# Linear attention with a GELU MLP behind it: the second group's output in seven products, and the last group's stores cut in halves

## The chip, the cores and the metric

The kernel runs on one core of a Trainium2 chip. The metric is the device time of one execution in microseconds. The five engines of the core run side by side: TensorE (PE in the profile) multiplies matrices into PSUM, VectorE (DVE) and ScalarE (ACT) work elementwise, GpSimd (POOL) does a few casts here, and SyncE (SP) issues most DMAs. Each works through its own queue of instructions in order and waits on semaphores for the others.

## What is computed

```python
# q, k, v: 8 batches, 8 heads, 576 rows, 64 wide
phi = lambda x: where(x > 0, x, exp(x) - 1) + 1
q_p, k_p = phi(q), phi(k)
kv  = einsum('bhsd,bhse->bhde', k_p, v)
z   = sum(k_p, axis=2)
x   = einsum('bhsd,bhde->bhse', q_p, kv) / (einsum('bhsd,bhd->bhs', q_p, z)[..., None] + 1e-06)
x   = x.transpose(0, 2, 1, 3).reshape(4608, 512)
h   = x @ w_in                      # 512 -> 2048
g   = gelu_tanh(h)
out = g @ w_out                     # 2048 -> 512
```

## The kernel before

**Tiling.** The 4608 rows are taken in nine groups. Groups 0 to 7 are the first 512 rows of batches 0 to 7; group 8 is made of the last 64 rows of all eight batches. `iteration(j)` does group j: `h` in 16 blocks of 128 features by 512 rows (four matmuls each, into one PSUM bank), a gelu per block on ScalarE into `g`, and then `o`, the product of `g` with `w_out`. The attention of a group that comes later (its exps, its kv, its division and its transposes) is done in between, so that TensorE is never without work.

**Two forms of o.** Groups 0 and 1 multiply plainly: per quarter of 128 rows, 16 matmuls with 512 columns (`o_mm`, line 723), and a copy to `o_sb` by ScalarE or VectorE (`finish`). In group 1 half of them stand after the first eight h, the other half after the last eight. Groups 2 to 8 cut `g` and `w_out` into two by two blocks and form `o` from seven products and not eight (`class Products`): each has 16 matmuls with 256 columns (`product`, line 770), some on sums of blocks of `g` (`s[0]`, `s[1]` and two blocks of `g` overwritten in place, line 752) and on differences of blocks of `w_out` (`w_sum` and one block of `w_out_sb` overwritten, `sum_w_out`, line 741). The results are put together by VectorE additions from PSUM (`plus`, line 830) and two ScalarE copies. Three of the products, 2, 4 and 3, are added by TensorE to a bank that already holds another one (`p`, `w`, `z`), so these banks stay taken for some time, and an addition that reads such a bank has to be done before TensorE adds to it again.

**PSUM.** There are six single banks (`ps_b`) for h, o, transposes and some of the attention, and one pair of banks (`ps_a`) for kv and for `n` of the attention, the numerator and denominator of one quarter of the rows (`nab`; `nab_in_banks` takes two single banks instead).

**The order.** Nothing is scheduled by the compiler: each engine executes in the order in which the program writes its instructions. `steps` in `iteration` lists the h blocks and products of a group, and after step number `slot` the function `run(j, slot)` calls what `at(j, slot, ...)` has put there. `plan_third` and `plan_fourth` put the attention of batches 2 and 3 into group 1 and the start of group 2:

- `linear_of` (VectorE, line 228) and `exp_of` (ScalarE, line 220) are the two branches of phi, `least_of` (VectorE, line 234) their minimum. The exp tiles `q_e` and `k_e` exist once each. `gelu_table` (line 418) brings ScalarE's gelu table back after exps.
- `least_q` takes the minimum for q and then issues four DMA transposes `qt<-q_p` on SP's queue (line 660); `transposed_x` issues one `xt<-xs` per quarter (line 683).
- `load_all_pairs` and `load_q` issue loads on SP's queue.
- `cast_v`, `kv_in_pair` and the `n` steps follow.
- `attention` of batch 3 stands in group 2 after slot 12 (line 328) and uses four single banks and the pair.

**Stores.** In groups 0 to 7 ScalarE's queue issues the stores of `o`. Group 8 stores through `store_rest` (line 834), alternately from ScalarE's queue and SP's: the left half of `o1`, all of `o2` (both column halves at once, after product 4), and the right half of `o1` in two pieces at the very end.

Of the kernel before, what the change touches and what calls it, by code (L numbers as in the profile page):

```python
# [16 lines left out]
def kernel(  # L17
# [28 lines left out]
    MM = d_ff // P  # L46
    E = D + 1
    N2 = d_model // 2
# [337 lines left out]
    xts, qts = {}, {}  # L386
# [126 lines left out]
    def at(j, slot, fn, *args):  # L513


        fill.setdefault((j, slot), []).append((fn, args))
# [73 lines left out]

    def plan_third():
        def n(c):
            transposed_x(2, c, nab(qts[2], 2, c))

        for i, name in enumerate("qk"):
            at(1, 2 + i, linear_of, name, 2)
            at(1, 7, exp_of, name, 2)
        at(1, 4, cast_v, 2)
        at(1, 7, gelu_table)
        at(1, 9, least_q, 2)  # L600
        at(1, 10, load_all_pairs, "k", k, 4)
        at(1, 11, least_of, "k", 2)
        at(1, 16, kv_in_pair, 2)
        for c in range(C):
            at(1, 18 + 2 * c, n, c)

    def plan_fourth():

        for name, b in (("k", 3), ("q", 3), ("k", 4)):
            at(1, 23, exp_of, name, b)  # L610
        at(1, 23, gelu_table)
        at(1, 24, linear_of, "k", 3)
        at(1, 25, linear_of, "q", 3)
        at(1, 26, least_of, "k", 3)
        at(1, 31, least_q, 3)
        at(2, 0, cast_v, 3)
        at(2, 4, kv_in_pair, 3)
        at(2, 5, linear_of, "k", 4)
        at(2, 5, least_of, "k", 4)
        at(2, 5, cast_v, 4)  # L620
        at(2, 8, linear_of, "q", 4)
        at(2, 15, exp_of, "q", 4)
        at(2, 16, exp_of, "k", 5)
        at(2, 19, least_q, 4)
        at(2, 22, linear_of, "k", 5)
        at(3, 0, least_of, "k", 5)
# [53 lines left out]
    def transposed_x(b, c, x):  # L680
        if b not in xts:
            xts[b] = pt.tile([P, NP, MAIN], BF16, name="xt")
        nc.sync.dma_start_transpose(out=xt_chunk(b, c), in_=x)
# [50 lines left out]
    def sum_w_out(ns):  # L734

        b11, b21 = (w_out_sb[:, 0, h] for h in ff)
        b12, b22 = (w_out_sb[:, 1, h] for h in ff)
        t1, t2, t4 = (w_sum[:, n] for n in range(3))
        sums = ((t1, b12, b11), (t2, b22, t1), (t4, b21, t2), (b12, b22, b12))
        for out, i0, i1 in sums[ns]:  # L740
            nc.vector.tensor_tensor(out, i0, i1, op=ALU.subtract)

# [2 lines left out]
    class Products:  # L745
# [5 lines left out]
        def subtract(self, out, i0, i1, op=ALU.subtract):  # L751
            nc.vector.tensor_tensor(out, i0, i1, op=op)  # L752

        def sums(self, ms):

            (a11, a12), (a21, a22) = [[h[:, ms] for h in t] for t in self.a]
            s1, s2 = (s[:, ms] for s in self.s)
            self.subtract(s1, a21, a22, ALU.add)
            self.subtract(s2, s1, a11)
            self.subtract(a21, a11, a21)  # L760

        def last_sum(self):

            self.subtract(self.a[0][0], self.a[0][1], self.s[1])

        def product(self, ps, lhs, rhs, first, ts=range(2)):

# [8 lines left out]
                        skip_group_check=True,  # L776
                    )

        def step(self, n):
            j = self.j  # L780
            (a11, a12), (a21, a22) = self.a
            (b11, b21), (t3, b22) = [[w_out_sb[:, d, h] for h in ff] for d in range(2)]
            t1, t2, t4 = (w_sum[:, i] for i in range(3))
            lo, hi = slice(0, N2), slice(N2, d_model)
            if n == 1 and j == B:
                ps = [bank("o_ps", [P, N2]) for _ in range(2)]
            elif n < 4:
                ps = bank("o_ps", [P, 2, N2])
            if n == 0:
                self.p = ps  # L790
                self.product(ps, a11, b11, True)
                self.o1 = pout.tile([P, 2, d_model], FP32, name="o_sb")
                self.o2 = pout.tile([P, 2, d_model], FP32, name="o_sb")
                nc.scalar.copy(self.o1[:, :, hi], ps)
            elif n == 1:
                self.z = ps
                self.product(ps, self.s[0], t1, True)
            elif n == 2:
                self.product(ps, self.s[1], t2, True)
                self.plus(self.o1[:, :, hi], ps, self.o1[:, :, hi])  # L800
            elif n == 3:
                self.w = ps
                self.product(ps, a21, t3, True)
                self.plus(self.o2[:, :, hi], ps, self.o1[:, :, hi])
                if j < B:
                    self.plus(self.o2[:, :, hi], self.z, self.o2[:, :, hi])
                else:
                    for t in range(2):
                        self.plus(self.o2[:, t, hi], self.z[t], self.o2[:, t, hi])
            elif n == 4:  # L810
                self.product(self.p, a12, b21, False)
                nc.scalar.copy(self.o1[:, :, lo], self.p)  # L812
                if j == B:
                    self.store(0, self.o1, lo)
            elif n == 5:
                self.product(self.w, a22, t4, False)
                self.plus(self.o2[:, :, lo], self.w, self.o1[:, :, hi])
                self.store(1, self.o2)
            elif j < B:
                self.product(self.z, a11, b22, False)  # L820
                self.plus(self.o1[:, :, hi], self.z, self.o1[:, :, hi])
                at(j + 1, 0, self.store, 0, self.o1)
            else:
                for t in range(2):
                    self.product(self.z, a11, b22, False, (t,))
                    self.plus(self.o1[:, t, hi], self.z[t], self.o1[:, t, hi])
                    self.store_rest(t, self.o1[:, t], hi)

        def plus(self, out, i0, i1):
            nc.vector.tensor_tensor(out, i0, i1, op=ALU.add)  # L830
# [17 lines left out]
    def iteration(j):  # L848
        xt = xts[j]
        if j < B:  # L850
            g = pg.tile([P, 2, MM, MAIN // 2], FP16, name="g")
        else:
            g = pg.tile([P, MM, 2, MAIN // 2], FP16, name="g").rearrange("p m a n -> p a m n")
        hs = [("h", m) for m in range(MM)]
        us = [range(m, m + 4) for m in range(0, MM, 4)]
        if j == 0:
            us[2:3] = range(8, 10), range(10, 12)
            steps = hs + [("o", t, u) for u in us for t in range(C)]
        elif j == 1:
            os = [[("o", t, u) for u in us[i : i + 2] for t in range(C)] for i in (0, 2)]  # L860
            steps = hs[:8] + os[0] + hs[8:] + os[1]
        else:
            products = Products(j, g)
            steps = [hs[i + n] for i in range(MM // 2) for n in (0, MM // 2)]
            steps += [("product", n) for n in range(7)]
            at(j, 7, products.sums, slice(0, 4))
            at(j, 15, products.sums, slice(4, 8))
            at(j, 16, products.last_sum)
        o_pss = {}
        for slot, step in enumerate(steps):  # L870
            if step[0] == "h":
                m = step[1]
                h_ps = h_begun.get(j, {}).get(m)
                if h_ps is None:
                    h_ps = bank("h_ps", [P, MAIN])
                    h_mm(h_ps, xt, m)
                gelu(j, g, m, h_ps)
            elif step[0] == "product":
                products.step(step[1])
            else:  # L880
                t, u = step[1:]
                if u.start == 0:
                    o_pss[t] = bank("o_ps", [P, d_model])
                o_mm(o_pss[t], g, t, u, half=(j, slot - 0.5))
                if u.stop == MM:
                    finish(j, t, o_pss[t])
            run(j, slot)
# [7 lines left out]
        plan_rest(m)  # L895
    for b in range(3, B + 1):
        plan_attention(b)
    at(1, 26, load_all_pairs, "v", v, 4)
    at(1, 26, load_q, 4)
    for b in range(5, B):  # L900
        at(b - 3, 1, load_all_pairs, "k", k, b)
        at(b - 3, 1, load_q, b)
# [3 lines left out]
        at(5, 1, load_rest, m + 2)  # L906
    for j in range(2, 7):
        at(j, 16, gelu_table)
    at(1, 4, sum_w_out, slice(0, 3))
    at(2, 0, sum_w_out, slice(3, 4))  # L910

    for j in range(B + 1):
        iteration(j)
# [30 lines left out]
```

## Time and profile before

| what | value |
|---|---|
| median of 8 runs | 273.5 us (273.27 to 273.77) |
| the profiled execution's own time | 273.47 us |
| its span, first to last instruction | 271.7 us |
| granted TensorE clock, mean | 0.997 |
| end of the last TensorE work in the chain of waits | 267.2 us |
| start of group 1's h in the chain / of group 2's | 47.58 us / 76.96 us |
| VectorE and ScalarE busy, share of the span | 58% and 61% |

The span is what the profiler saw from the first to the last instruction; the time lies 1.8 us above it. A line of the timeline reads: start, length in us, engine, source line, operation, output and input with their shapes, count, and in brackets how long the engine had been idle and what ended that. "PEld" is TensorE's weight load, "SPq" and "ACTq" are the issuing of DMAs. A matmul's record reaches some tenths of a microsecond past the start of the next one, since matmuls are pipelined; the distance between starts is what a matmul costs in a stream.

### The profile page before, as it was taken

To read this page: it belongs to the slowest core of one execution; us is meant where nothing else is said; L and a number is where in the kernel's file an instruction comes from. 1 tells how busy PE (TensorE), PEld (TensorE's weight loads), DVE (VectorE), ACT (ScalarE), POOL (GpSimd) and SP (SyncE) were. 2 spreads that over 40 slices of the span, in tenths; PEclk is the share of its full clock that TensorE was granted. 3 is DMA by queue.
4 is the path that set the end of the run, shared out by engine and by line. 5 is a ranking of instruction groups with operands and counts; after the bars stand their busy time and mean duration, and the time that the engine had idled before them with its cause. 6 is when DMAs were issued, how large, how long until landed. Compare 5 with 4: busy or idle time off the path is not lost.

```text
span 271.7 us, 5804 instructions
## 1 busy us (share of the span) xinstructions
PE 264.2 (97%) x2465; PEld 166.1 (61%) x2485; DVE 157.7 (58%) x251; ACT 166.4 (61%) x224; POOL 15.0 (6%) x21
## 2 busy tenths in 40 slices
PE   8999999999999999999999999999999999999993
PEld 2584455445444686558655865587458645864682
DVE  3860186944688966788738874682367236522342
ACT  4768878795888683668366926672764365048600
POOL 3047301000000000000000000000000000000000
PEclk9999999999999999999999999999999999999998
DMA  7999999985999986992698463328121403030004
GB/s 247 401 406 396 410 406 402 400 345 126 201 334 259 398 155 178 304 314 58 178 370 245 97 177 101 60 51 166 75 58 41 166 10 73 7 154 0 2 0 156
DMA packets 59497, 53.85 MB, mean 198 GB/s; under 512 B 35664, under 2 KB 45392, under 8 KB 59472
## 3 DMA queue, kind: packets, MB, share of 16 engines
q1 hardware_dynamic: 56736, 44.57, 55.1%
q10 hardware_dynamic: 2736, 8.91, 9.0%
q8 instruction: 19, 0.31, 0.5%
q14 instruction: 6, 0.05, 0.1%
HBM read 36.70 MB, written 9.44 MB: 170 GB/s over the span
## 4 chain that ended last, share of the span: by engine, by line
PE 93%; DMA 3%; SPq 1%; DVE 1%; issue 1%; ACT 0%
PE h_ps L390 46%; PE o_ps L770 32%; PE o_ps L723 10%; DMA v_x<-in_v_dram 3%; PE n_ps L328 1%; PE n_ps L250 1%; PE kv_ps L250 1%; PE n_ps L266 1%; PE t_ps L383 1%; SPq L94 1%; SPq L99 0%; PE t_ps L541 0%; DVE vp L239 0%; DVE xs L373 0%; DVE o_sb L830 0%
## 5 line engine op out<-in xcount | busy, mean ns | idle before, releaser
L390 PE MATMUL h_ps<-xt,w_in_sb 128*128 128x512 bf16 (+1 forms) x609 | 127.8, 361 | 1.0
L405 ACT ACTIVATE g<-h_ps 128x512 f16<-128x512 f32 x144 | 87.0, 616 | 62.2 <-PE h_ps L390 59.8
L390 PEld LDWEIGHTS <-w_in_sb 128*128 128x128 bf16 x628 | 58.1, 98 | 62.2
L770 PEld LDWEIGHTS <-g 128*128 128x128 f16 x560 | 54.8, 98 | 7.8
L770 PE MATMUL o_ps<-w_out_sb,g 128*128 128x256 f16 x448 | 52.3, 273 | 0.0
L830 DVE TENSOR_TENSOR o_sb<-o_ps,o_sb 128x512 f32<-128x512 f32 (+1 forms) x37 | 24.4, 662 | 29.3 <-PE o_ps L770 28.5
L752 DVE TENSOR_TENSOR s<-g 128x1024 f16<-128x1024 f16 x14 | 9.7, 691 | 38.3 <-ACT g L405 38.3
L723 PE MATMUL o_ps<-w_out_sb,g 128*128 128x512 f16 x128 | 29.4, 379 | 0.0
L284 DVE TENSOR_TENSOR xs<-n_ps,r 128x384 bf16<-128x384 f32 (+2 forms) x43 | 25.4, 592 | 1.5
L770 PE MATMUL o_ps<-w_sum,s 128*128 128x256 f16 x224 | 25.6, 273 | 0.0
L770 PEld LDWEIGHTS <-s 128*128 128x128 f16 x224 | 21.9, 98 | 2.5
L723 PEld LDWEIGHTS <-g 128*128 128x128 f16 x128 | 12.1, 98 | 13.3
L812 ACT COPY o_sb<-o_ps 128x512 f32<-128x512 f32 x7 | 4.1, 585 | 22.2 <-PE o_ps L770 22.2
L220 ACT ACTIVATE k_e<-k_x 128x2304 bf16<-128x2304 f32 (+1 forms) x9 | 17.2, 1908 | 0.8 <-DMA k_x<-in_k_dram 0.7
L228 DVE TENSOR_SCALAR q_p<-q_x 128x2048 bf16<-128x2048 f32 (+1 forms) x9 | 9.9, 1102 | 13.0 <-DMA q_x<-in_q_dram 13.0
L220 ACT ACTIVATE q_e<-q_x 128x2048 bf16<-128x2048 f32 (+1 forms) x9 | 15.5, 1719 | 2.7 <-DMA q_x<-in_q_dram 2.7
L770 PE MATMUL o_ps<-w_sum,g 128*128 128x256 f16 x112 | 13.4, 273 | 0.0
L228 DVE TENSOR_SCALAR k_p<-k_x 128x2304 bf16<-128x2304 f32 (+1 forms) x9 | 11.0, 1218 | 4.1 <-DMA k_x<-in_k_dram 4.1
L234 DVE TENSOR_TENSOR q_p<-q_p,q_e 128x2048 bf16<-128x2048 bf16 (+1 forms) x9 | 9.9, 1101 | 3.2 <-ACT q_e L220 3.0
L234 DVE TENSOR_TENSOR k_p<-k_p,k_e 128x2304 bf16<-128x2304 bf16 (+1 forms) x9 | 11.0, 1221 | 1.3 <-ACT k_e L220 1.0
L418 ACT ACT_TABLE_LOAD x9 | 11.5, 1283 | 0.2
L283 DVE RECIPROCAL r<-n_ps 128x6 f32<-128x6 f32 (+2 forms) x43 | 8.2, 190 | 5.5 <-PE n_ps L266 5.5
(61 smaller groups left out, 156.5 us busy)
## 6 DMA issues: line engine op xcount, KB each, us to landing
out_dram<-o_sb ACTq DMA_DIRECT2D x16, 512.0 KB, 4.5
k_x<-in_k_dram SPq DMA_DIRECT2D x7, 1152.0 KB, 6.8
v_x<-in_v_dram SPq DMA_DIRECT2D x7, 1152.0 KB, 12.3
q_x<-in_q_dram SPq DMA_DIRECT2D x6, 1024.0 KB, 12.5
w_st<-in_moe_w_in_dram SPq DMA_DIRECT2D x3, 1024.0 KB, 13.2
q_x<-in_q_dram SPq DMA_DIRECT2D x4, 512.0 KB, 8.7
w_st<-in_moe_w_out_dram SPq DMA_DIRECT2D x2, 1024.0 KB, 12.5
w_st<-in_moe_w_out_dram SPq DMA_DIRECT2D x4, 512.0 KB, 11.3
```

The lines of the kernel that those rows point to most:

```text
L220: nc.scalar.activation(o, i, AF.Exp)
L228: nc.vector.tensor_scalar(o, i, 1.0, 1.0, op0=ALU.add, op1=ALU.max)
L234: nc.vector.tensor_tensor(p, p, e, op=ALU.min)
L283: nc.vector.reciprocal(r, n_v[heads + (D,)])
L284: nc.vector.tensor_tensor(x_v, n_v[heads + (slice(0, D),)], r[heads + (None,)].to_broadcast(shape + [D]), op=ALU.mult,)
L390: nc.tensor.matmul(h_ps[:, ts], lhsT=w_in_sb[:, c, P * m : P * (m + 1)], rhs=xt[:, c, ts], start=(c == 0), stop=(c == KM - 1), skip_group_ ...
L405: nc.scalar.activation(g_v, h_v, AF.Gelu_apprx_tanh)
L418: nc.scalar.preload_act_table_set("gelu_apprx_tanh_and_others")
L723: nc.tensor.matmul(o_ps, lhsT=g[:, t // 2, m, P * (t % 2) : P * (t % 2 + 1)], rhs=w_out_sb[:, :, m, :], start=(m == 0), stop=(m == MM - 1),)
L752: nc.vector.tensor_tensor(out, i0, i1, op=op)
L770: nc.tensor.matmul(ps[t] if type(ps) is list else ps[:, t, :], lhsT=lhs[:, m, P * t : P * (t + 1)], rhs=rhs[:, m, :], start=(first and m = ...
L830: nc.vector.tensor_tensor(out, i0, i1, op=ALU.add)
```

## The change

- **Group 1's o in seven products.** `Products` is used for groups 1 to 8. In group 1 products 1 and 7 stand after the eighth h, and products 2, 6, 5, 4, 3 after the sixteenth. Product 7 needs the block difference `third_sum`, which in group 1 is put into `s[0]` (freed again for its own sum later). The sums follow at slots 13, 17 and 19.
- **The exps of batch 2** stay after the eighth h, that is ahead of the copy of product 1 on ScalarE's queue, with k ahead of q.
- **The attention of batches 2 and 3 moves**: `kv_in_pair` of batch 2 from slot 16 to 12, its `n` steps to slots 15, 17, 18 and 18, the last one in two single banks; exps of batch 3 and of k of batch 4 between slots 17 and 18; `linear_of` k of batch 3 from 24 to 12, of q from 25 to 21; `least_of` k of batch 3 to slot 22, which is the end of the group, and `least_q` of batch 3 to group 2's slot 0. (With plain o the group had slots up to 31, with products it has 22.)
- **The differences of w_out** are taken at slots 1 and 7 of group 1, in another order.
- **The last group's stores**: the right half of `o2` is stored as soon as it has been added up, ahead of product 2's copy, and the left half after product 4.

```diff
     def plan_third():
         def n(c):
-            transposed_x(2, c, nab(qts[2], 2, c))
-
-        for i, name in enumerate("qk"):
-            at(1, 2 + i, linear_of, name, 2)
-            at(1, 7, exp_of, name, 2)
+            transposed_x(2, c, (nab_in_banks if c == 3 else nab)(qts[2], 2, c))
+
+        at(1, 1, sum_w_out, slice(0, 2))
+        at(1, 2, linear_of, "k", 2)
+        at(1, 3, linear_of, "q", 2)
         at(1, 4, cast_v, 2)
+        at(1, 7, exp_of, "k", 2)
+        at(1, 7, exp_of, "q", 2)
         at(1, 7, gelu_table)
+        at(1, 9, least_of, "k", 2)
         at(1, 9, least_q, 2)
-        at(1, 10, load_all_pairs, "k", k, 4)
-        at(1, 11, least_of, "k", 2)
-        at(1, 16, kv_in_pair, 2)
-        for c in range(C):
-            at(1, 18 + 2 * c, n, c)
+        at(1, 9, load_all_pairs, "k", k, 4)
+        at(1, 12, kv_in_pair, 2)
+        for c, slot in enumerate((15, 17, 18, 18)):
+            at(1, slot, n, c)
 
     def plan_fourth():
 
-        for name, b in (("k", 3), ("q", 3), ("k", 4)):
-            at(1, 23, exp_of, name, b)
-        at(1, 23, gelu_table)
-        at(1, 24, linear_of, "k", 3)
-        at(1, 25, linear_of, "q", 3)
-        at(1, 26, least_of, "k", 3)
-        at(1, 31, least_q, 3)
+        at(1, 12, linear_of, "k", 3)
+        at(1, 17, exp_of, "k", 3)
+        at(1, 18, exp_of, "q", 3)
+        at(1, 18, exp_of, "k", 4)
+        at(1, 18, gelu_table)
+        at(1, 21, linear_of, "q", 3)
+        at(1, 22, least_of, "k", 3)
         at(2, 0, cast_v, 3)
+        at(2, 0, least_q, 3)
...
-        sums = ((t1, b12, b11), (t2, b22, t1), (t4, b21, t2), (b12, b22, b12))
+        sums = ((t1, b12, b11), (b12, b22, b12), (t2, b22, t1), (t4, b21, t2))
...
+        def third_sum(self, ms, in_place=True):
+
+            a11, a12, a21, a22, s1, s2 = self.quarters(ms)
+            self.s3 = self.a[1][0] if in_place else self.s[0]
+            self.subtract(a21 if in_place else s1, a11, a21)
...
+            if name == 1:
+                self.p = new()
+                self.product(self.p, a11, b11, True)
...
+            elif name == 7:
+                self.w = new()
+                self.product(self.w, self.s3, t3, True)
+            elif name == 2:
+                self.product(self.p, a12, b21, False)
+                nc.scalar.copy(self.o1[:, :, lo], self.p)
+                if j == B:
+                    self.store(0, self.o1, lo)
+            elif name == 4:
+                self.product(self.w, a22, t4, False)
+                self.plus(self.o2[:, :, lo], self.w, self.o1[:, :, hi])
+                self.store(1, self.o2, lo if j == B else slice(0, d_model))
...
+            both = {6, 7} <= set(self.done)
+            if name in (6, 7) and both:
+                self.plus(self.o2[:, :, hi], self.w, self.o1[:, :, hi])
+            if name in (5, 6, 7) and both and 5 in self.done:
                 if j < B:
                     self.plus(self.o2[:, :, hi], self.z, self.o2[:, :, hi])
                 else:
                     for t in range(2):
                         self.plus(self.o2[:, t, hi], self.z[t], self.o2[:, t, hi])
...
+                    self.store(1, self.o2, hi)
...
+        products = Products(j, g) if j else None
+        early, late = slice(0, MM // 4), slice(MM // 4, MM // 2)
...
         elif j == 1:
-            os = [[("o", t, u) for u in us[i : i + 2] for t in range(C)] for i in (0, 2)]
-            steps = hs[:8] + os[0] + hs[8:] + os[1]
+            steps = hs[:8] + [("product", n) for n in (1, 7)]
+            steps += hs[8:] + [("product", n) for n in (2, 6, 5, 4, 3)]
+            at(1, 7, products.third_sum, early, False)
+            at(1, 7, products.third_sum, late, False)
+            at(1, 7, sum_w_out, slice(2, 4))
+            at(1, 13, products.sums, early)
+            at(1, 17, products.sums, late)
+            at(1, 19, products.last_sum)
         else:
-            products = Products(j, g)
             steps = [hs[i + n] for i in range(MM // 2) for n in (0, MM // 2)]
-            steps += [("product", n) for n in range(7)]
-            at(j, 7, products.sums, slice(0, 4))
-            at(j, 15, products.sums, slice(4, 8))
+            steps += [("product", n) for n in (1, 5, 6, 7, 2, 4, 3)]
...
-    at(1, 26, load_all_pairs, "v", v, 4)
-    at(1, 26, load_q, 4)
+    at(1, 19, load_all_pairs, "v", v, 4)
+    at(1, 19, load_q, 4)
...
-    at(1, 4, sum_w_out, slice(0, 3))
-    at(2, 0, sum_w_out, slice(3, 4))
```

Products 1 to 7 in the new numbering are, in the order of groups 2 to 8 before, steps 0, 4, 6, 5, 1, 2 and 3: the order of those groups is unchanged.

More of the change, by code (lines that the diff above doesn't have):

```diff
@@ L752, in subtract, with quarters, last_sum @@
             nc.vector.tensor_tensor(out, i0, i1, op=op)
+        def quarters(self, ms):
+            (a11, a12), (a21, a22) = [[h[:, ms] for h in t] for t in self.a]
+            return a11, a12, a21, a22, *(s[:, ms] for s in self.s)
         def sums(self, ms):
-            (a11, a12), (a21, a22) = [[h[:, ms] for h in t] for t in self.a]
-            s1, s2 = (s[:, ms] for s in self.s)
+            a11, a12, a21, a22, s1, s2 = self.quarters(ms)
             self.subtract(s1, a21, a22, ALU.add)
             self.subtract(s2, s1, a11)
-            self.subtract(a21, a11, a21)
-        def last_sum(self):
-            self.subtract(self.a[0][0], self.a[0][1], self.s[1])
+        def third_sum(self, ms, in_place=True):
+            a11, a12, a21, a22, s1, s2 = self.quarters(ms)
+            self.s3 = self.a[1][0] if in_place else self.s[0]
+            self.subtract(a21 if in_place else s1, a11, a21)
+        def last_sum(self, ms=slice(0, MM // 2)):
+            a11, a12, a21, a22, s1, s2 = self.quarters(ms)
+            self.subtract(a11, a12, s2)
         def product(self, ps, lhs, rhs, first, ts=range(2)):
@@ L777, in product, with step @@
                     )
-        def step(self, n):
+        def step(self, name):
             j = self.j
@@ L784, in step, with new @@
             lo, hi = slice(0, N2), slice(N2, d_model)
[L785 to L791, printed above, removed]
+            self.done = getattr(self, "done", ()) + (name,)
+            def new():
+                if name == 5 and j == B:
+                    return [bank("o_ps", [P, N2]) for _ in range(2)]
+                return bank("o_ps", [P, 2, N2])
@@ L792, in step @@
+            if name == 1:
+                self.p = new()
+                self.product(self.p, a11, b11, True)
                 self.o1 = pout.tile([P, 2, d_model], FP32, name="o_sb")
                 self.o2 = pout.tile([P, 2, d_model], FP32, name="o_sb")
[L794 to L804, printed above, removed]
+                nc.scalar.copy(self.o1[:, :, hi], self.p)
+            elif name == 5:
+                self.z = new()
+                self.product(self.z, self.s[0], t1, True)
+            elif name == 6:
+                v = new()
+                self.product(v, self.s[1], t2, True)
+                self.plus(self.o1[:, :, hi], v, self.o1[:, :, hi])
+            elif name == 7:
[10 more added lines that the diff above has]
+                self.store(1, self.o2, lo if j == B else slice(0, d_model))
+            elif name == 3 and j < B:
+                self.product(self.z, a11, b22, False)
+                self.plus(self.o1[:, :, hi], self.z, self.o1[:, :, hi])
+                at(j + 1, 0, self.store, 0, self.o1)
+            elif name == 3:
+                for t in range(2):
+                    self.product(self.z, a11, b22, False, (t,))
+                    self.plus(self.o1[:, t, hi], self.z[t], self.o1[:, t, hi])
+                    self.store_rest(t, self.o1[:, t], hi)
@@ L809, in step @@
                         self.plus(self.o2[:, t, hi], self.z[t], self.o2[:, t, hi])
[L810 to L827, printed above, removed]
+                    self.store(1, self.o2, hi)
         def plus(self, out, i0, i1):
@@ L859, in iteration @@
         elif j == 1:
-            os = [[("o", t, u) for u in us[i : i + 2] for t in range(C)] for i in (0, 2)]
-            steps = hs[:8] + os[0] + hs[8:] + os[1]
+            steps = hs[:8] + [("product", n) for n in (1, 7)]
[6 more added lines that the diff above has]
+            at(1, 19, products.last_sum)
         else:
-            products = Products(j, g)
             steps = [hs[i + n] for i in range(MM // 2) for n in (0, MM // 2)]
-            steps += [("product", n) for n in range(7)]
-            at(j, 7, products.sums, slice(0, 4))
-            at(j, 15, products.sums, slice(4, 8))
+            steps += [("product", n) for n in (1, 5, 6, 7, 2, 4, 3)]
+            for slot, ms in ((7, early), (15, late)):
+                at(j, slot, products.sums, ms)
+                at(j, slot, products.third_sum, ms)
             at(j, 16, products.last_sum)
```

## The prediction

> **What bounds the kernel now.** I read the page's engine shares, then the chain of waits in order of time, then the timeline of the two places that the change touches.
>
> ```profile
> PE 264.2 (97%) x2465; PEld 166.1 (61%) x2485; DVE 157.7 (58%) x251; ACT 166.4 (61%) x224; POOL 15.0 (6%) x21
> PE 93%; DMA 3%; SPq 1%; DVE 1%; issue 1%; ACT 0%
> 54.49 6.91 PE o_ps L723 x32
> ...
> 70.92 6.04 PE o_ps L723 x28
> ...
> 93.00 12.23 PE o_ps L770 x112
> ...
> 267.24 0.42 DVE o_sb L830
> ```
>
> The chain (start, length, what) is TensorE from 12 us to 267.2 us without a gap. Time that TensorE saves ends the kernel earlier, provided nothing new makes it wait. Group 1's o is two blocks of 32 matmuls of 512 columns, one here (6.91 us) and one split by a fill; a later group's o is 112 matmuls of 256 columns in 12.23 us. The engines that could make TensorE wait, ScalarE and VectorE, look half idle, but these are averages. The second view is the timeline around the end of group 1:
>
> ```profile
> 54.53 0.60 ACT L405 ACTIVATE g<-h_ps 128x512 f16<-128x512 f32 x1 [0.27 <-PE h_ps L390]
> 55.15 1.28 ACT L220 ACT_TABLE_LOAD   x1
> 60.38 1.28 ACT L418 ACT_TABLE_LOAD   x1
> ...
> 74.21 1.35 DVE L234 TENSOR_TENSOR k_p<-k_p,k_e 128x2304 bf16<-128x2304 bf16 x1
> 75.60 2.12 ACT L220 ACTIVATE k_e<-k_x 128x2304 bf16<-128x2304 f32 x1
> 77.74 1.28 ACT L418 ACT_TABLE_LOAD   x1
> 78.02 6.33 SPq L660 DMA_TRANSPOSE qt<-q_p  x4
> 81.09 4.23 ACT L405 ACTIVATE g<-h_ps 128x512 f16<-128x512 f32 x8 [0.42 <-ACT o_sb L696]
> 88.93 0.66 PE L328 MATMUL n_ps<-kv,qt 64*128 64x65 bf16 x32
> 105.27 0.69 DVE L830 TENSOR_TENSOR o_sb<-o_ps,o_sb 128x512 f32<-128x512 f32 x1 [1.05 <-PE o_ps L770]
> 105.87 1.35 DVE L228 TENSOR_SCALAR k_p<-k_x 128x2304 bf16<-128x2304 f32 x1
> ```
>
> Two things are to be seen. ScalarE does gelus up to 55.13, then exps between two table loads until 61.66. And exp k of batch 4 starts at 75.60, just as VectorE's min of batch 3 ends (75.56): both use the one k_e buffer. TensorE can run only six PSUM banks ahead of the gelus.
>
> **Products against plain matmuls.** Removed: 64 matmuls at 6.91/32 = 215.9 ns, 13.82 us. Added: 112 at 12.23/112 = 109.2 ns, 12.23 us. That is **-1.59 us**. Here a rule of the Trainium skill speaks against the change: "TensorE: Matmul & The Clock Gate", section "Back-to-back issue gap", gives streams of weight load plus matmul as about 81 ns at 128 columns and 131 ns at 512. A straight line between makes 256 columns about 98 ns, so as an estimate 64 x 131 = 8.4 us would become 112 x 98 = 11.0 us, a loss of 2.6. The rows have the stream itself in this kernel, both sizes at a granted clock of 0.997; I take the rows.
>
> **What group 1 waits for in the new order.** Times are those at which the records let a matmul start (0.16 us before the chain's). The products begin where the plain o began, 54.33. Product 1 now wants block 7 of g as its 8th weights, at 55.09; its gelu ends at 55.13, so 0.2 us are lost. They are part of the next wait. ScalarE then goes through the exps as before (k ahead of q, the same two lengths) to 61.66, copies product 1 (0.58, pitch 0.51 as in a pair of copies) and does the gelu of h8 from about 62.2 to 62.8. Meanwhile TensorE does products 1 and 7 (3.49), h8 to h10 (2.60), kv (0.86: 62.27 to 63.35 in the chain, less one matmul) and h11 (0.86): ready for h12 at 62.15. With products 1 and 7 holding two banks and h8 to h11 four, h12 waits for h8's gelu, in the built program too: 62.86, **0.71 us**. Before, plain o filled this time.
>
> From there VectorE, which got some 9 us of sums and additions in this group, is the next to be late. Its first sum of new halves waits for h11's gelu (about 64.4). Then come the second sum (to 65.84), reciprocal and division of n(0) (0.24 + 0.69, to 66.7). n(1) uses the same pair of banks, so it starts at 66.82 where TensorE is ready at 66.55: **0.27 us**. In the same way I follow the queue: n(1)'s division to 68.2, two sums to 69.5 (product 6 wants them at 69.6, no loss), n(2) and n(3) to 71.5, two additions to 72.8. Product 4 adds to the bank that the second reads and is ready at 72.76: **0.1 us**. Product 3 comes out even (its operand's sum and z's addition end at 73.9 and 74.6, it is ready at 74.6). The other additions, and the third sums for product 7 (done at 55.9, wanted at 56.3 and 56.7), are hidden under TensorE. The q transposes on SP's queue go out at 61.7 instead of 59.7; with the 2.4 us that they took, the first lands at 64.1, and n(0) comes at 64.6. The load of k of batch 4 is queued behind them (66.9 for 65.0), lands some 6.4 us later and is wanted at 78. The x transposes end as before (last issue about 71.5 for 72.15).
>
> So group 1 is 54.33 + 12.23 + 6.92 (eight h) + 0.86 + 0.92 (four n) + 1.08 (waits) = 76.34 against 76.80 recorded: **-0.46 us**.
>
> **Group 2 begins with a late ScalarE.** Least k of batch 3 now stands in VectorE's queue behind the addition for product 3, the last of the group. By the rows of group 3 such an addition starts 0.21 us after the group's end G, and the next operation 0.60 after that. So min k runs from G+0.82 to G+2.18, exp k of batch 4 (same buffer) to G+4.34, the table to G+5.64, then a store issue and the first gelu (0.42 + 0.60): G+6.66. TensorE has six free banks, and wants h6 of group 2 at G+6.05 by the old trace (82.85 - 76.80); it waits for that gelu: G+6.71. **+0.66 us**, whatever G is. Before, ScalarE was done 1.2 us ahead at this place. The cover that is gone is the min being early.
>
> Least q of batch 3 comes after it: its four transposes leave at about 81.0 to 84.8, not 78.02 to 83.15, and k, q and v of batch 5 (SP's next) about 1.6 us later, which have over 3 us to spare. Attention of batch 3 wants the last transpose at about 89.55. Its landing is not in the trace; bounds: 2.4 us as at 59.67 (87.2, no loss) and 7.4 as the slowest of the four at 78 to 83 (92.2, 2.65 us). Nearest is the last of those, 5.3 us, with loads and stores in front; now only the two o stores (1 MB) stand there. I take **+0.1 us**.
>
> **The tail.** The page has, and the timeline's end:
>
> ```profile
> out_dram<-o_sb SPq DMA_DIRECT2D x2, 128.0 KB, 2.6
> out_dram<-o_sb SPq DMA_DIRECT2D x1, 256.0 KB, 3.8
> ...
> 266.21 2.02 SPq L834 DMA_DIRECT2D out_dram<-o_sb  x2
> ```
>
> The 128 KB stores took 2.2 us (issued at 264.36 with an empty queue) and 2.9 us (the last, at 267.69, landing 270.6 with 1.1 us of closing down behind). In between 256 KB went to each queue at 266.2, and the DMA was busy at some 370 GB/s until 269.4. The edit sends half of them about 2.7 us earlier, when nothing flows. One more issue of 0.56 us on each queue falls into idle time before 264.36. The last store then finds its queue emptier: 2.2 for 2.9, **-0.7 us** (bounds 0.3, if the other late half is still in its way, and 0.9). TensorE and VectorE end as before.
>
> **Sum.** -0.46 + 0.66 + 0.1 - 0.7 = -0.4. Against the profiled execution's 273.47 (span 271.7, 1.8 around it; the median 273.5 is the same) this gives **273.1 us**.
>
> **Rivals.** First: the saving holds. If the waits of group 2 don't arise (the exp starts earlier, or gelus free banks sooner) and half of group 1's waits go, -1.05 - 0.7 gives 271.7; with only the smaller group 1 waits gone, 272.6. For it: each wait is a difference of a few tenths between sums of a dozen durations. Against: the min stands behind the last addition in VectorE's order, and the trace shows exp starting with min's end.
>
> Second, on the other side: the transposes of q of batch 3 decide in place of ScalarE. They leave SP 3 us later for the first, 1.6 for the last, and attention needs all four. From a landing of 4.75 us for the last, TensorE waits; from 5.7 on the kernel is slower than before by more than 0.5. At 6.4 us (the middle of the two slower in the trace) it is 91.2 - 89.55 = 1.65 more: 274.8. For it: the trace's own landings of 4.8 to 7.4. Against: by 81.4 the loads in front are through.
>
> Third: the change doesn't do what it says in its first part, h does not run ahead: only four h fit, and that is in the sum already; without the tail's gain it leaves +0.3, 273.8.
>
> **Chances.** My sum 0.5 (own range 272.6 to 273.7), the saving holds 0.27, transposes 0.15, no tail gain or another wait 0.08. What a measurement of this kernel can tell from no change is about 0.2%, 0.55 us: faster is below 272.9, slower above 274.0. From the sum's case 0.17 faster and 0.33 same; from the first rival 0.25 and 0.02; from the rest 0.03 same and 0.20 slower. Range 272.2 to 274.3: below it lies the better half of the first rival, above it the bad half of the second.
>
> **What would show it.** Right: group 1's o at 109 ns a matmul; TensorE idle about 0.7 us at the fifth h after the products, waiting for a gelu, and 0.6 at h6 of group 2; exp k of batch 4 starting with min's end near 78.5; the last store landing in about 2.2 us. Wrong: no idle at h6 (first rival); an idle of TensorE before L328 near 89 (second); a last landing still near 2.9.

## The result, and the profile after

The changed kernel takes **272.48 us** (median of 11 runs, 272.28 to 273.45) against 273.56 of the kernel before on the same chips (31 runs): a ratio of 0.9966, interval 0.9958 to 0.9974. Its profiled execution took 272.62 us with a span of 270.8 (before: 273.47 and 271.7). The page's engine shares and the shares of the chain of waits:

```profile
PE 262.2 (97%) x2513; PEld 170.2 (63%) x2533; DVE 165.4 (61%) x263; ACT 165.5 (61%) x224; POOL 14.5 (5%) x21
PE 89%; DMA 5%; ACT 2%; DVE 1%; SPq 1%; issue 1%; ACTq 0%
```

TensorE is busy 2.0 us less, but its share of the chain falls from 93% to 89%: ScalarE comes into the chain, and DMA has 5% of it for 3%. The chain itself, from the start of group 1 on (start, length, what):

```profile
47.63 1.09 PE h_ps L390 x9
...
54.54 3.59 PE o_ps L782 x32
...
62.42 0.60 SPq L663
63.02 0.06 issue
63.08 4.04 DMA qt<-q_p
...
67.57 1.75 PE o_ps L782 x16
69.32 0.47 PE n_ps L266 x8
69.78 7.06 PE o_ps L782 x64
76.85 0.02 issue
76.87 0.14 DVE o_sb L851
77.01 0.47 issue
77.48 1.36 DVE k_p L234
78.84 0.02 issue
78.86 2.13 ACT k_e L220
...
82.94 6.20 PE h_ps L390 x28
89.15 0.60 PE n_ps L328 x32
...
93.15 12.23 PE o_ps L782 x112
...
255.13 12.24 PE o_ps L782 x112
```

Blocks of h (h0 to h15) and quarters (n(0) to n(3)) are counted from 0. Two stretches are no longer TensorE's. At 63 to 67 us a transpose of q of batch 2 is waited for, and from 76.85 to 82.9 VectorE's addition, k's least, exp k and the table load stand one behind the other. The view of waits says the same, with the total, the count and the longest in us:

```profile
ACT k_e L220 <- DVE k_p L234: 5.8, 1, 5.8
PEld L266 <- DMA qt<-q_p: 0.9, 1, 0.9
PE h_ps L390 <- ACT g L405: 0.5, 1, 0.5
```

ScalarE stood idle for 5.8 us until k's least was done. TensorE's weight load for n(1) waited for the transpose, and its matmul for h12 waited for a gelu.

Group 1 starts anywhere from 47.5 to 48.2 us in the executions of kernels whose work is the same up to there. So kernels are compared by three pieces of its own chain: **group 1** (the start of its h to the end of its last product, or of plain o), **group 2 before o** (from there to the start of group 2's o), and **tail** (the end of TensorE's last matmul to the end of the span). The tails use spans to 0.01 us, 271.67 before and 270.77 after; the expectations took spans to 0.1 and so have 4.48 and 3.75 for 4.45 and 3.74. What lies between the second and the third piece took 174.2 us in before and after alike.

| kernel | group 1 | group 2 before o | tail |
|---|---|---|---|
| before | 29.38 | 16.04 | 4.45 |
| after | 29.21 | 16.31 | 3.40 |

Before, group 1 runs from 47.58 to 76.96 and group 2's o starts at 93.00; after, 47.63, 76.84 and 93.15. The last matmul ends at 267.22 and 267.37. So seven products and their new order bring -0.17 in group 1, and +0.27 comes back in group 2. The whole gain of this execution, -1.05 us, is in the tail. Other executions of the same order of work (experiments 2 and 10) have 28.97 and 29.03 for group 1, so that groups 1 and 2 together come to 0.15 and 0.08 below before, for 0.10 above it here: near nothing in all three.

### The profile page after: what moved, and what is told of

It is laid out like the page before. It is cut to its first block, busy times and chain, and to the rows that moved or that the text cites. A ratio compares the mean times of both kernels' runs of the same rounds, so it can differ in the third digit from the quotient of the medians.

```text
span 270.8 us, 5916 instructions
## 1 busy us (share of the span) xinstructions
PE 262.2 (97%) x2513; PEld 170.2 (63%) x2533; DVE 165.4 (61%) x263; ACT 165.5 (61%) x224; POOL 14.5 (5%) x21
## 4 chain that ended last, share of the span: by engine, by line
PE 89%; DMA 5%; ACT 2%; DVE 1%; SPq 1%; issue 1%; ACTq 0%
PE h_ps L390 43%; PE o_ps L782 36%; PE o_ps L726 5%; DMA v_x<-in_v_dram 3%; DMA qt<-q_p 1%; PE n_ps L328 1%; PE n_ps L250 1%; PE n_ps L266 1%; ACT k_e L220 1%; PE kv_ps L250 1%; PE t_ps L383 1%; SPq L94 1%; DVE k_p L234 1%; ACT L418 0%; SPq L99 0%
## 5 line engine op out<-in xcount | busy, mean ns | idle before, releaser
L782 PEld LDWEIGHTS <-g 128*128 128x128 f16 x624 | 60.9, 98 | 9.0 <-ACT g L405 0.2
L782 PE MATMUL o_ps<-w_out_sb,g 128*128 128x256 f16 x496 | 58.2, 273 | 0.0
L851 DVE TENSOR_TENSOR o_sb<-o_ps,o_sb 128x512 f32<-128x512 f32 (+1 forms) x42 | 27.9, 665 | 29.6 <-PE o_ps L782 28.8
L755 DVE TENSOR_TENSOR s<-g 128x1024 f16<-128x1024 f16 x18 | 12.4, 691 | 39.1 <-ACT g L405 39.0
L782 PE MATMUL o_ps<-w_sum,s 128*128 128x256 f16 x256 | 29.3, 273 | 0.0
L782 PEld LDWEIGHTS <-s 128*128 128x128 f16 x272 | 26.6, 98 | 3.0
L782 PE MATMUL o_ps<-w_sum,g 128*128 128x256 f16 x128 | 15.3, 272 | 0.0
L726 PE MATMUL o_ps<-w_out_sb,g 128*128 128x512 f16 x64 | 15.1, 379 | 0.0
L755 DVE TENSOR_TENSOR s<-s,g 128x1024 f16<-128x1024 f16 x16 | 11.1, 692 | 0.5
L239 DVE CAST vp<-v_x 128x2304 bf16<-128x2304 f32 (+1 forms) x9 | 11.0, 1224 | 0.5 <-DMA v_x<-in_v_dram 0.4
```

The costliest lines, as they stand in the source:

```text
L239: fn(out=vp_paired(b)[:, :, us, 0:D].rearrange("p j u d -> p u j d"), in_=ld["v", b][:, us].rearrange("p u (j d) -> p u j d", d=D),)
L726: nc.tensor.matmul(o_ps, lhsT=g[:, t // 2, m, P * (t % 2) : P * (t % 2 + 1)], rhs=w_out_sb[:, :, m, :], start=(m == 0), stop=(m == MM - 1),)
L782: nc.tensor.matmul(ps[t] if type(ps) is list else ps[:, t, :], lhsT=lhs[:, m, P * t : P * (t + 1)], rhs=rhs[:, m, :], start=(first and m = ...
```

## Experiments

Ratios are to the kernel before, run beside each on the same chip; it took 273.55 us beside experiments 1, 2, 7 and 8, 273.75 beside 3, 4, 9 and 10, and 273.22 beside 5, 6, 11 and 12.

**1. Half stores alone.** The kernel before, with the stores of the last group as after:

```diff
                         self.plus(self.o2[:, t, hi], self.z[t], self.o2[:, t, hi])
+                    self.store(1, self.o2, hi)
...
-                self.store(1, self.o2)
+                self.store(1, self.o2, lo if j == B else slice(0, d_model))
```

> The kernel before with only the last group's stores cut in halves. Theory 1 (the waits in groups 1 and 2 eat what the seven products save, and all of the gain is the tail): about 1.0 us below the kernel before, 272.5 us, as fast as the whole change; the last TensorE work ends where it did before (267.2 us) and the last store lands about 2.0 us after its issue and not 2.9. Theory 2 (the products keep a good part of their 1.59 us, the tail brings only the 0.7 us of the shorter landing or less): 272.8 to 273.2 us.

Measured: 272.79 us (272.71 to 272.95), ratio 0.9972 [0.9961, 0.9983]. Group 1 29.38, tail 3.60. That is the greater part of the gain, from two of the change's lines. Groups 1 and 2 are as before, so all of it is in the tail. It falls between the numbers of the two theories.

**2. All but the half stores.** The changed kernel with `o2` stored whole, as before:

> The changed kernel with the last group's stores whole, as before. Theory 1: 0 to 0.2 us above the kernel before, 273.5 to 273.7 us, with TensorE idle at h12 of group 1, ahead of n of quarter 1, and at h6 of group 2. Theory 2: 0.3 us or more below the kernel before.

Measured: 272.73 us (272.47 to 273.31), ratio 0.9974 [0.9964, 0.9983]: as much again, as theory 2 has it. Yet group 1 (28.97) and group 2 (16.30) together are only 0.15 shorter than before. Its tail is 3.74 instead of 4.45, with the same stores at the same distance from TensorE's end. What differs shows in the view of DMA from 266 us on (GB/s in slices of 0.185 us, then queues and issues). The kernel before:

```profile
GB/s 371 332 28 0 0 0 0 122 332 410 399 377 365 454 354 371 382 388 249 28 22 22 22 0 0 0 0 0 0 0 0 0 0 0 0 0 0 0 0 0
...
q14 instruction: 1, 0.01, 0.6%
...
out_dram<-o_sb SPq DMA_DIRECT2D x1, 256.0 KB, 3.8
out_dram<-o_sb ACTq DMA_DIRECT2D x1, 256.0 KB, 3.2
...
out_dram<-o_sb SPq DMA_DIRECT2D x1, 128.0 KB, 2.9
```

and experiment 2, where the same stores are issued 0.43 us later:

```profile
GB/s 172 376 371 399 100 0 0 0 0 0 299 432 399 399 432 399 399 344 376 382 354 39 0 0 0 0 0 0 0 0 0 0 0 0 0 0 0 0 0 0
...
out_dram<-o_sb SPq DMA_DIRECT2D x1, 256.0 KB, 3.0
out_dram<-o_sb ACTq DMA_DIRECT2D x1, 256.0 KB, 2.4
...
out_dram<-o_sb SPq DMA_DIRECT2D x1, 128.0 KB, 2.2
```

Before, the rate falls to 22 to 28 GB/s for the last 0.7 us: that is the rate of one DMA engine of the 16 (some 400 / 16 = 25). So one engine is still working off its part, and the stores land only as it gets through. In the same window queue 14 fetched one block of instructions, in one packet. In the window of half a microsecond about it, 267.0 to 267.5, the last number of its line is its packet's share of the time of 16 engines:

```profile
q14 instruction: 1, 0.01, 8.5%
```

That is 0.085 x 16 x 0.5 = 0.68 us of one engine, which is the lag. In experiment 2 and after, queue 14's last block came at 240 to 246 us. Queue 14 is taken for VectorE's: the change gives VectorE 338 instructions of all kinds for 325 (counted in the built programs), so the same block boundary would be met earlier.

Laid out by cause, the tail is

| | block fetched at 267 us | block fetched by 246 us |
|---|---|---|
| stores whole | 4.45 (before) | 3.74 (2) |
| stores in halves | 3.60 (1) | 3.40 (after) |

The earlier block is worth 0.71 with whole stores and 0.20 with halves. The half stores are worth 0.85 and 0.34; by the view of experiment 1 the rate no longer ends in a stretch at one engine's rate, though its block falls in the same place. Experiments 7 to 12, all with half stores and the block by 246 us, have tails of 3.40 or 3.41.

**3 and 4. That cause by itself.** The kernel before, and that of experiment 1, each with 13 tiny VectorE memsets of a tile that nothing reads, so that VectorE has 338 instructions and the work is unchanged:

```diff
+    pad = const.tile([P, 8], BF16, name="pad")
+    for _ in range(13):
+        nc.vector.memset(pad, 0.0)
```

> The kernel before, with 13 tiny VectorE memsets of a tile that nothing reads added at its start, so that VectorE's instruction count is 338, as after the change, and nothing else differs. Theory 1 (the last stores of the kernel before wait for an instruction transfer, some 8 KB on one DMA engine, that falls at 267 us, and the 13 more instructions of the change put it at about 243 us): 272.8 us, about 0.7 less than before; no instruction transfer after 260 us; 3.75 us from TensorE's last instruction to the end of the span in place of 4.48. Theory 2 (the gain of the run with whole stores came from the products, the transfer does nothing): 273.5, no change, 4.48 us.

> The kernel before with the half stores alone, and the same 13 memsets: VectorE's count as after the change, but the order of the matmuls and the mapping steps as before. Theory 1 (the whole gain is in the tail, and the products, h run ahead and k before q add up to nothing): 272.5 us, the same as the changed kernel within 0.15, with 3.4 us from TensorE's last instruction to the end. Theory 2 (products and order keep something of their own): 272.8 to 273.0, 0.3 or more above the changed kernel.

Measured: 275.26 us (275.07 to 275.48), ratio 1.0052 [1.004, 1.0064], and 274.95 (274.75 to 276.03), 1.0047 [1.0031, 1.0064]. Both totals missed every theory. Group 1 starts 2.3 us late in both, at 49.95 and 49.88, and from there on they do as theory 1 says: group 1 29.39 and 29.38, tails 3.87 and 3.44, and queue 14's block between 240 and 250 us, so it does follow VectorE's count. I first put the late start down to the memsets, which stand at the front of VectorE's queue.

**5 and 6. The memsets moved amid the products** of groups 2 to 7, where VectorE idles:

```diff
                 self.plus(self.o1[:, :, hi], ps, self.o1[:, :, hi])
+                for _ in range(0 if j == B else 3 if j == 2 else 2):
+                    nc.vector.memset(pad, 0.0)
```

> The kernel before with the same 13 tiny VectorE memsets, now amid its products (three behind an addition of group 2, two behind one of each of groups 3 to 7, where VectorE idles), so that the start is as before. Theory 1 (the instruction transfer at 267 us holds up the last stores, and 13 more VectorE instructions put it earlier): 272.9 us, 0.6 to 0.7 less than before, 3.75 to 3.9 us from TensorE's last instruction to the end in place of 4.48, group 1's start to TensorE's last instruction unchanged at 219.64. Theory 2 (no effect): 273.6, 4.48. That a kernel gets faster by doing more would leave only the place of the transfer as cause.

> The kernel before with the half stores and the 13 memsets amid the products: the tail of the changed kernel without its new order. Theory 1 (the whole gain of the change is the tail): 272.5 us, the changed kernel's within 0.15, tail 3.4 to 3.5 us. Theory 2 (products and order keep something): 272.8 or more.

Measured: 275.18 us (275.12 to 275.19), ratio 1.0071 [1.0057, 1.0085], and 274.71 (274.56 to 274.8), 1.0054 [1.0042, 1.0067]. The totals miss again, with group 1 starting at 49.84 and 49.87. So it is not the memsets: nothing but the tile `pad` differs there before group 2. The last section says what it does. The tails are the test, and they are 3.88 and 3.44, as in experiments 3 and 4. The view of DMA of experiment 5, over the same 266 to 273.4 us:

```profile
GB/s 0 0 0 0 0 0 0 0 0 0 177 360 332 354 194 0 0 0 0 0 310 421 387 365 366 387 376 343 338 338 343 271 6 0 0 0 0 0 0 0
...
out_dram<-o_sb SPq DMA_DIRECT2D x1, 256.0 KB, 3.1
out_dram<-o_sb ACTq DMA_DIRECT2D x1, 256.0 KB, 2.4
```

The work is that of the kernel before, the stores are whole, and no engine lags: 3.1 and 2.4 us for 3.8 and 3.2. With the block of instructions elsewhere the tail is 0.57 shorter. A control that leaves the tile's place in memory alone wasn't run.

**7. The wait at group 2's h6.** The changed kernel with k's least of batch 3 taken ahead of the last product:

```diff
-        at(1, 21, linear_of, "q", 3)
-        at(1, 22, least_of, "k", 3)
+        at(1, 21, least_of, "k", 3)
+        at(1, 22, linear_of, "q", 3)
```

> The changed kernel with the minimum for k of batch 3 moved one step up on VectorE's queue, ahead of the last addition of group 1, and the linear part of q of batch 3 moved behind it. Theory 1: exp k of batch 4 starts about 1.7 us earlier (77.1 for 78.86), the idle time of 0.65 us at h6 of group 2 is gone, and attention of batch 3 then comes close to the landing of its last q transpose, which may cost 0 to 0.3: 0.3 to 0.65 us below the changed kernel, 271.9 to 272.2 us. Theory 2 (h6 is not what costs, or another wait takes its place at once): no change against the changed kernel.

Measured: 272.75 us, ratio 0.9966 [0.9955, 0.9976], in two clusters: 272.14 to 272.43 and 272.75 to 273.34. The median is no lower than after (272.48, with the same ratio), as theory 2 has it. The profiled execution is one of the lower cluster (272.15). Its chain has neither VectorE nor ScalarE after the products:

```profile
69.65 7.04 PE o_ps L782 x64
...
76.96 4.05 PE h_ps L390 x18
81.01 0.71 PE kv_ps L250 x72
...
82.09 6.64 PE h_ps L390 x30
88.73 0.60 PE n_ps L328 x32
```

Group 2 before o is 16.04, as before the change: the wait is gone, for 0.27 us. But group 1 is shorter too, 28.86 for 29.21, which this edit can't do. The view of DMA shows why. After, queue 8 in the window from 64 to 65 us, and the rate from 64.5 to 66.6 us (slices of 0.0525 us):

```profile
q8 instruction: 1, 0.02, 7.6%
...
GB/s 273 258 278 273 278 195 93 24 5 1 0 0 0 0 0 0 0 0 0 0 5 20 10 10 10 15 10 10 10 5 10 10 15 25 0 0 0 0 0 49
```

A block of 0.02 MB of instructions on queue 8 comes at 64.4 us, just as the second of the four transposes of q moves its data, and takes 0.076 x 16 = 1.2 us of one engine. Most of the transpose is through by 64.9, but one engine's part follows at some 10 GB/s from 65.6 to 66.2 us, and n(1), which needs this transpose, finds it landed 4.0 us after its issue. In experiment 7 that block comes at 62.4 us, ahead of the second transpose; the four land in 2.4 us (median), and n(1) doesn't wait for them. The other traces agree: in experiments 2 and 10 the block comes at 62.6 and 65.1 us, and the first transpose takes 3.2 us in the one, the second 3.8 in the other; in experiments 8, 11 and 12 it comes at about 70 us, behind all four, and each of them lands in 2.4 us. Whether the upper cluster is the other order wasn't seen, as it has no profile.

**8. The wait at n(1).** The changed kernel with q's exp and least of batch 2 ahead of k's, and kv one slot later:

```diff
+        at(1, 7, exp_of, "q", 2)
         at(1, 7, exp_of, "k", 2)
-        at(1, 7, exp_of, "q", 2)
...
+        at(1, 9, least_q, 2)
         at(1, 9, least_of, "k", 2)
-        at(1, 9, least_q, 2)
...
-        at(1, 12, kv_in_pair, 2)
+        at(1, 13, kv_in_pair, 2)
```

> The changed kernel with q ahead of k again in the exps and minima of batch 2, and kv of batch 2 after the fourth run-ahead h and not after the third, so that it does not wait for the later k. Theory 1: the q transposes leave SP at about 59.8 for 61.7 us and have landed before n of quarter 1, which then waits for VectorE only (about 66.8 for 67.16); kv falls into the wait at h12. 0.2 to 0.4 us below the changed kernel, 272.1 to 272.3 us. Theory 2 (k ahead of q is what keeps TensorE running, as the order intends): kv waits for k, and the kernel is 0.3 to 1.0 us slower than the changed one.

Measured: 272.33 us (272.18 to 272.4), ratio 0.9953 [0.9942, 0.9965]. Group 1 28.88, group 2 before o 16.31. The transposes leave at 59.8 for 61.7, and their landing no longer matters: -0.33 us against after in group 1, and -0.15 against the execution of after in experiment 10. Mapping k ahead of q, with kv a slot earlier, was a small loss, not a gain.

**9 and 10. Both, and the changed kernel beside it.**

> The changed kernel with the least of k of batch 3 one slot earlier (its wait at group 2's h goes) and exp and least of q ahead of k for batch 2 with kv later (the wait of n(1) for the transposes goes). Theory 1 (the two waits add up): start of group 1 to TensorE's last instruction 218.8 us against 219.7 after the change, 271.6 to 271.9 us. Theory 2 (the time given free by one is taken by a later wait for transposes or gelus, as nothing of the other engines is shorter): 219.1 to 219.5 us, 272.1 to 272.4.

> The changed kernel itself, on the same chip as the three others, to compare them with: 272.5 us within 0.2, group 1's start to TensorE's last instruction 219.7 us within 0.15.

Measured: both 272.06 us (271.97 to 272.19), ratio 0.9936 [0.9924, 0.9947]; after 272.56 (272.42 to 272.68), 0.9953 [0.9941, 0.9965]. All runs of the one are below all of the other. Group 1 and group 2: 28.87 and 16.04, against 29.03 and 16.31 in this execution of after. The two gains add, to 219.13 us from group 1's start to TensorE's last instruction (after: 219.74, and 219.55 in experiment 10), theory 2's number. Its reason was not the right one, though: 218.8 had counted 0.35 us of experiment 7 for the edit that was the luck of the instruction block.

**11 and 12. The next wait.** In experiment 9 the chain runs over ScalarE from 54.8 to 63.05 us: gelu, table load, exp q, exp k, table load, the copy of product 1 (0.59) and the gelu that h12 waits for. The copy was given to VectorE in group 1:

```diff
-                nc.scalar.copy(self.o1[:, :, hi], self.p)
+                (nc.vector.tensor_copy if j == 1 else nc.scalar.copy)(self.o1[:, :, hi], self.p)
```

> The run with both waits taken away, and group 1's first copy of product 1 given to VectorE in place of ScalarE, where it stands for 0.59 us between the second table load and the gelu that h12 waits for. Theory 1 (ScalarE's chain sets h12): group 1 0.2 to 0.4 us shorter, 271.75 us. Theory 2 (the copy pushes k's least on VectorE and with it kv, which TensorE meets first): no change within 0.1, 272.05, with the wait at kv in place of the one at h12.

> The run with both waits taken away once more, on the chip of the three others, to compare the last with: 272.05 us within 0.15.

Measured: 271.67 us (four runs from 271.46 to 271.75, one of 272.59), ratio 0.9948 [0.9935, 0.9961], against 271.89 (271.86 to 272.1), 0.9953 [0.9941, 0.9966]. Group 1 is 28.44, 0.43 shorter than 28.87, but group 2 before o is 16.31 for 16.04. The chain of experiment 11 there:

```profile
68.89 7.05 PE o_ps L782 x64
75.94 4.32 PE h_ps L390 x20
80.26 0.75 PE kv_ps L250 x72
81.01 0.67 SPq L663
...
84.57 3.94 DMA qt<-q_p
88.50 0.05 issue
88.55 0.30 PE n_ps L328 x8
```

TensorE now meets the fourth transpose of q of batch 3: the place that the prediction's second rival named. But it meets it because this one is late: it leaves at 84.57 us and takes 3.9 us to land, at 88.5, while in experiment 12 it leaves at 84.73 and takes 2.5, landing at 87.2. There the attention starts at 88.45; in experiment 11 group 1 ends 0.48 us earlier (75.94 for 76.42), and an attention 0.48 earlier, as an estimate at 87.97, would still come behind 87.2. Whether the edit or the one execution made this landing late isn't shown. What is left, 0.16 us, is in the spread of the runs. Experiments 9 and 11 beat both kernels.

## Why the prediction was right, and where not

The forecast was 273.1 us, 272.2 to 274.3. The time lies in the range, but 0.6 below the forecast, just below the likeliest case's own 272.6 to 273.7, and below the 272.9 under which the prediction counts it as faster (0.42 of its chances). The waits arose where they were named, so it isn't the first rival. Group 1 came out 0.29 slower than forecast, group 2 with its transposes 0.49 faster, and the tail 0.35 better; that the first two errors nearly cancel is luck.

- **Products, -1.59.** Held: group 1's products are at 7.06/64 = 110.3 ns a matmul against 109.2 from the row, and their three stretches in the chain come to 12.40 us for 12.23. By the estimate from the Trainium skill ("TensorE: Matmul & The Clock Gate", "Back-to-back issue gap") the products would have been 2.6 us longer than the plain matmuls; they are shorter, for the plain matmuls take 215.9 ns by the row of before and not the page's 131. The row was the right source.
- **The waits of group 1, back to -0.46.** h12's start was predicted as 62.86 and is recorded at 62.86: ScalarE sets it, as said. TensorE was ready later than worked out (idle for 0.5 us there, not 0.71), which costs nothing at this place. n(1)'s was predicted as 66.82, from VectorE's division; it is recorded at 67.16. **This step failed**: "with the 2.4 us that they took" was taken for the transposes' landing, and one of them took 4.0 us. VectorE's division ended at 66.70, as the prediction had it. So n(1) came 0.34 late, and group 1 ended 0.29 behind the forecast, at -0.17. Product 4 and product 3 cost nothing that the chain shows.
- **Group 2's h6, +0.66.** The mechanism was right and the size too great. By the records group 2's first h starts at 76.67; k's least ran from 77.48 and exp k ended 4.32 us behind that h, as worked out (0.82 and 4.34). The term of 0.42 for a store issue between the table load and the first gelu was wrong: the issue stands ahead of the table load and has 0.09 us of the chain. So the gelu ended at 82.91, and +0.27 was left. Experiment 7 takes just that away.
- **The transposes of batch 3, +0.1.** Nothing: L328 starts as soon as h is through. Two errors cancel in this, which is luck: the last transpose left at 86.3 us, not 84.8, and took 2.4 us, not some 5. It landed at 88.7, half a microsecond ahead of L328 at 89.15, so nothing was lost, with little to spare. As a rival they were not wrong in kind; they decide in the execution of experiment 11, for 0.27. (That rival's own sum is off: -0.46 + 0.66 - 0.7 + 1.65 from 273.47 is 274.6, not 274.8.)
- **The tail, -0.7.** Measured -1.05, outside the bounds of 0.3 and 0.9. The half stores do what was said, and the last one lands in 2.0 us instead of 2.9. But the reason given, a queue emptied earlier, leaves something out: without the lagging engine behind an instruction block the half stores are worth 0.34, and with it 0.85. The trace of before had that engine, as four slices at 22 to 28 GB/s and one packet of queue 14; I had read the 370 GB/s ahead of them and not what came behind. By experiments 1 and 2 either cure takes most of the loss (0.85 and 0.71); taken together (1.05) they aren't worth their sum.

Between group 1's start and TensorE's last instruction, +0.30 was predicted and +0.10 measured (-0.09 in experiment 10). The prediction's chain of before is TensorE's without a gap from 14.6 us, not from 12, which doesn't bear on the change. The products were in fact a saving whose gain other engines take back: of 1.59 us, 0.17 was left in group 1, and with the waits at n(1) and h12 taken away (experiments 9 and 11) 0.94.

## What to carry to other kernels

When TensorE's work shrinks, follow ScalarE's and the transposes' queue from the same place: with the waits at n(1) and h6 removed, the next one to look at was h12's, and removing that (0.43 us) met a transpose that took 0.27 back. At the end of a kernel look at the DMA rate in fine slices, not at the mean: a tail at one engine's rate means that a single engine is late, and then smaller stores, sent earlier, help more (0.85 us here, against 0.34 without the late engine). Compare executions from a fixed event of the chain and not by their totals; the start alone varied more here than the effect of most edits.

## What the runs showed of the hardware

**Blocks of instructions share the DMA engines with the data.** One of about 8 KB at 267 us lengthened the last stores by some 0.7 us, and one of 16 KB at 64.4 us a transpose from 2.4 to 4.0 us, each, by the rates that are left, by making one of 16 engines late. Queue 14's last block moved from 267 to 245 us with 13 more VectorE instructions (experiments 3 to 6), so an edit of the count can move one. Queue 8's moved without that: it came at 64.4 and at 65.1 us in two executions of the same kernel (after and experiment 10).

**A tile of 16 bytes in front of the landing places goes with a lower DMA rate.** In experiments 3 to 6 the tile `pad` moved every tile allocated behind it, among them all landing places of loads, by 32 bytes: the first of these begins at byte 63,008 of a partition instead of 62,976, by the built programs (the one a multiple of 32, the other of 512). The table by stage, whose last two columns are the busy share of the DMA engines and their rate in GB/s, has for the kernel before

```profile
12.00:20.00 8.00, 7.15 (x158) 6.28 (x149) 5.55 (x17) 4.67 (x10) 3.77 (x4) 1.00 1.06 402
20.00:30.00 10.00, 9.95 (x47) 4.53 (x47) 1.23 (x1) 8.11 (x15) 5.68 (x3) 1.00 1.06 400
30.00:47.00 17.00, 17.00 (x185) 9.39 (x183) 10.05 (x17) 13.85 (x16) 3.12 (x3) 1.00 1.05 405
```

and for experiment 5

```profile
12.00:20.00 8.00, 7.04 (x166) 6.08 (x159) 5.76 (x17) 4.27 (x10) 2.73 (x4) 1.00 1.06 373
20.00:30.00 10.00, 9.89 (x52) 4.47 (x50) 0.13 (x1) 8.04 (x15) 6.71 (x4) 1.00 1.06 374
30.00:47.00 17.00, 15.95 (x165) 8.18 (x164) 10.35 (x16) 12.88 (x14) 3.12 (x3) 1.00 1.06 382
```

The DMA engines are fully busy in both, and move 6 to 7% less. The loads of the first 47 us then set the start of group 1, 2.3 us later. That it is the address of the landing places and not that of another tile moved with them is likely, but no run separates the two. A tile of 16 bytes cost more than twice what the whole change brings.
